# Attention's products in 64x64 tiles of the TensorE array, with dense K and Q

## The chip, the cores and the metric

The kernel runs on one core of a Trainium2 chip. The metric is the device time in microseconds of one execution; the kernel before has a median of 934.84 us over three runs (930.62 to 936.06).

## What is computed

Three stages follow one another: a delta-rule linear attention over 4 batches x 8 heads x 768 tokens x 48 features, a first MoE layer (384 to 1024 and back, SoLU with a layer norm), and a second (384 to 2048 and back, squared ReLU), each over 3072 tokens, all in float32.

```python
def attention(q, k, v, beta):                  # B, H, S, D = 4, 8, 768, 48
    k_n = k / (norm(k) + 1e-6)
    state = zeros(B, H, D, D)
    for t in range(S):
        y[:, :, t] = einsum('bhd,bhde->bhe', q[:, :, t], state)
        v_old = einsum('bhde,bhd->bhe', state, k_n[:, :, t])
        state += beta[:, :, t] * einsum('bhd,bhe->bhde', k_n[:, :, t], v[:, :, t] - v_old)
h = x @ w_in; s = h * softmax(h); x = layernorm(s) * g_ln @ w_out      # first MoE
r = max(x @ w_in2, 0); out = (r * r) @ w_out2                          # second MoE
```

## The kernel before

The sequence of a head is cut into 12 chunks of 64 tokens; 4 batches x 12 chunks are 48 steps, and two steps are one tile of 128 tokens, 24 tiles in all. The 8 heads stand as 4 pairs p, one head h = 0 or 1 of a pair in each half of the 128 partitions (64 tokens of a chunk, or 48 features and 16 unused rows). The unread products of a step, those that don't need the state, are these:

- **E** (`e_tile`, products at L684): K times [Q, K] of the chunk for all heads. K and Q of one step are a load of 96 rows (two heads of 48 features, no gap) x 512 columns from `kine`. Before the products, K is copied into a block-diagonal tile `kbd` or `ez`, one head's 64 columns at a time, each multiplied by a column of ones and zeros (`hm`): on ACT at L673, for half of the first tiles on DVE at L663. Four products of 96x128 weights and 128 moving columns follow, one for each pair, into one PSUM bank (`p_ep`; other free banks for the first seven tiles). ACT takes K x K out as `g` (L693) and DVE the masked K x Q as `m` (L718); `g` goes to DRAM (`gscr`).
- **Inversion** (`inversion`): the 64x64 triangular systems of 7 groups of tiles (2 to 4 tiles each), solved in halves of 32 after a transposing way through DRAM, one system on each of many partitions. Group 0 is on DVE, groups 1 to 6 on POOL (GpSimd); L881 scales the data that come in, L900 and L917 are the steps, L942 scales the result, which goes out to `tscr`.
- **Preparation** (`prep`): loads V (`vt`), the inverses as a block-diagonal `tbd`, and K, Q again in a layout of 64 rows per head with zero rows (`kin`, `kql`, 512 KB a tile). 32x32 products at L1037 and L1050 fill the lower corner of each inverse; they use `p_ep`, and ACT copies it out (L1057, L1068). POOL scales V by the norms (L1079).
- **z** (`zstep`): T times [m, K] of a step, four products of 128x128 weights and 112 columns into `p_z` (L1098), copied out by ACT as `zs` (L1109).

The **chain** (`chain`) is what is read in order, step after step: products of K, Q with the state (L1139, L1140, 48x64 tiles of the array into `p_a` and `p_o`), DVE `r` (L1171), products with `zs` (L1154, L1155), DVE `s` (L1182), ACT `xt` (L1188). A finished tile goes into the first MoE: transposes (L1207), `p_h` (L1218), `p_tr` (L1320), `p_x` (L1340). The second MoE (L1483, L1527) comes last, when all of that is done.

The order on each engine is not that of the code: a planner (`Plan`) takes every operation with an engine, a cost, the keys that it reads and writes, and a priority, and lists them by a list scheduling; `BANKS` names the keys of the PSUM banks. The five engines issue in exactly that order; SyncE (SP) issues all loads and stores. A semaphore wait holds back what stands behind it on its engine. `warm` puts 20 products of a 128x128 identity with itself (L821) on PE between the first E products and the first preparation; they stand behind a late step of inversion 0 in the plan (`late_step`), but read none of its data.

Of the kernel before, what the change touches and what calls it, by code (L numbers as in the profile page):

```python
# [18 lines left out]
P = 128  # L19
C = 64  # L20
# [94 lines left out]
class Plan:  # L115
# [9 lines left out]
    BANKS = {("A", "ep"), ("A", "z"), ("A", "a"), ("A", "o"), ("h", 0), ("h", 1), ("tr",), ("x1",)}  # L125
# [150 lines left out]
def tile_delta_moe_moe(  # L276
# [3 lines left out]
    kin: bass.AP,  # L280
# [45 lines left out]
    hm = cpool.tile([D2, 2], F32, name="hm")  # L326
    idle = cpool.tile([P, 16], F32, name="idle")
# [3 lines left out]
    fac = cpool.tile([P, NT], F32, name="fac")  # L331

# [11 lines left out]
    pool.memset(hm, 1.0)  # L344
    for h in range(2):
        pool.affine_select(
            out=hm[:, h : h + 1],
            in_=hm[:, h : h + 1],
            pattern=[[0, 1]],
            base=1 - D if h else D,  # L350
            channel_multiplier=1 if h else -1,
            compare_op=ALU.is_gt,
            fill=0.0,
        )
# [11 lines left out]
    make_identity(nc, ident)  # L366
# [18 lines left out]
    kbd_ = bufs(ap_, [P, NP, P], "kbd", 2)  # L385
    g_ = bufs(ap_, [P, 2, NP, C], "g", 2)
    sq_ = bufs(ap_, [P, NP, 3, 16], "sq", 2)
    nrm_ = bufs(ap_, [P, GS, NP], "nrm", 3)
    kql_ = bufs(ap_, [P, 2, NP, P], "kql", 2)
    vt_ = bufs(ap_, [P, 2, NP, D], "vt", 2)  # L390
    tbd_ = bufs(ap_, [P, 2 * NP, P], "tbd", 2)
# [17 lines left out]
    p_ep = psA.tile([P, 512], F32, name="p_ep")  # L409
    p_z = psA.tile([P, 512], F32, name="p_z")  # L410
    p_a = psA.tile([P, 512], F32, name="p_a")
    p_o = psA.tile([P, 512], F32, name="p_o")
    p_h = ps1.tile([P, F1], F32, name="p_h")
    p_tr = ps1.tile([P, 512], F32, name="p_tr")
    p_x1 = ps1.tile([P, 512], F32, name="p_x1")
# [7 lines left out]
    for t in (*tbd_, *s_, *g12_):  # L423
        pool.memset(t, 0.0)
# [149 lines left out]

    def rsqrt(y, x, t, n, r, w, prio):
# [38 lines left out]
    def e_tile(t, prio):  # L614
# [15 lines left out]
        for i in range(2):  # L630
            st = 2 * t + i
            kb, kkb = kbd_[i], [("A", "kbd", i)]
            kq, kkq = kqe_[st % 3], [("A", "kqe", st % 3)]
            bank, kep = p_ep, [("A", "ep")]
            if t < LA:

                if st % 6 < 4:
                    kb, kkb = half(ez_[st % 6 // 2], st % 2), [("ezh", st % 6)]
                bank, kep = (
                    (p_h[:, 0:512], [("h", 0)]),  # L640
                    (p_h[:, 512:], [("h", 1)]),
                    (p_tr, [("tr",)]),
                    (p_x1, [("x1",)]),
                    (p_ep, [("A", "ep")]),
                    (p_a, [("A", "a")]),
                    (p_o, [("A", "o")]),
                )[st % (7 if t < T2 else 4)]
# [8 lines left out]
            dma(lambda kq=kq: kq[0:D2], lambda st=st: kine[:, st], (), kkq, prio - 1, D2 * 2048)  # L656
            for h in range(2):
                s = slice(h * C, h * C + C)
                en = "dve" if h and t < T2 else "act"
                fn = (  # L660
                    act.mul
                    if en == "act"
                    else lambda o, x, y: v.tensor_tensor(  # L663
                        out=o,
                        in0=x,
                        in1=y.unsqueeze(2).to_broadcast([D2, NP, C]),
                        op=ALU.mult,
                    )
                )
                add(  # L670
                    en,
                    {"act": c_act(256, True) + 0.09, "dve": c_dve(256)}[en],
                    lambda kq=kq, kb=kb, h=h, s=s, fn=fn: fn(  # L673
                        kb[0:D2, :, s], kq[0:D2, :, C:P], hm[:, h : h + 1]
                    ),
                    kkq,
                    [(*k, h) for k in kkb],
                    prio,
                )
            gp = bank.rearrange("q (p c) -> q p c", p=NP)  # L680
# [5 lines left out]
            r = [*kkq, *((*k, h) for k in kkb for h in range(2))]  # L686
            if kkb[0][0] == "ezh":
                r.append(("ez", st % 6 // 2))
            add("pe", 0.88, mm, r, kep, prio)
# [76 lines left out]
    def gammas(g, prio):  # L766
# [34 lines left out]
        gt = p_z[:, NP * 112 : NP * 112 + HB]  # L801
# [6 lines left out]
        add("pe", 0.22, mm, [kbe], [("A", "z")], prio)  # L808
        add("act", c_act(HB), lambda: act.copy(gm, gt), [("A", "z")], [kgm], prio)

    last_inv = []

    late_step = []

    def warm(n, prio):

        for _ in range(n):

            def mm():
                for i in range(4):  # L820
                    pe.matmul(p_o[:, i * P : i * P + P], ident, ident, start=True, stop=True)  # L821

            add("pe", 0.9, mm, (), [("A", "o")], prio, after=late_step)

    def inversion(g, en, prio):
# [65 lines left out]
        for j in range(1, HB - 1):  # L891
            nr = HB - 1 - j
            for q, (c0, c1) in enumerate(((0, min(j, s1)), (s1, j))):
# [34 lines left out]
                if en == "pool" and run > 0.75:  # L928

                    fn = lambda: pool.memset(idle, 0.0)  # L930
                    brk = [add("pool", 0.1, fn, (), [("idle",)], prio, after=[last])]
                    run = 0.0
# [40 lines left out]
    def prep(t, prio):  # L973
# [7 lines left out]
        kq, vt, tb, t2, g12 = kql_[b], vt_[b], tbd_[b], t2_[b], g12_[b]  # L981
# [18 lines left out]
        for hb in (0, 2, 1, 3):  # L1000
            o = hb * HB
            last = dma(
                lambda o=o: tb[o : o + HB, :, o : o + HB],
# [19 lines left out]
        dma(lambda: kq, lambda: kin[:, 2 * t : 2 * t + 2], (), [("A", "kql", b, i) for i in range(2)], prio - 1, P * 4096)  # L1023

        for i, (bank, kp) in enumerate(((p_ep, "ep"), (p_a, "a")) if t == 0 else ((p_ep, "ep"),)):
# [7 lines left out]
            def mm1(us=us, yp=yp):  # L1033
                for u in us:
                    for h in range(2):
# [4 lines left out]
                            tb[o : o + HB, u, o : o + HB],  # L1040
# [20 lines left out]
            for h in range(2):  # L1061
                o = h * C
                for e in range(2):
# [5 lines left out]
                            tb[o + HB : o + C, us[0] + e : us[-1] + 1 : 2, o : o + HB],  # L1069
# [12 lines left out]
                in1=nrm_[g % 3][:, s0 : s0 + 2].unsqueeze(3).to_broadcast([P, 2, NP, D]),  # L1082
                op=ALU.mult,
            ),
            [("A", "nrm", g % 3, s) for s in (s0, s0 + 1)],
# [25 lines left out]
    def chain(st, prio):  # L1111
# [17 lines left out]
        def lower(h):  # L1129
            return slice(h * C, h * C + C)  # L1130
# [565 lines left out]
```

## Time and profile before

| | before |
|---|---|
| median of 3 runs | 934.84 us |
| the profiled execution | 934.67 us |
| its span in the trace | 932.7 us |
| busy: PE / DVE / ACT / POOL | 864.9 / 519.5 / 487.3 / 365.2 us |
| DMA | 101.75 MB, 109 GB/s mean |

PE is TensorE's matmul, PEld its weight load, SPq the queue of SyncE that issues DMAs. A matmul of float32 leaves two records in the trace, so an E step of four products has 8. Records of matmuls overlap, since they are pipelined: the pace is read from one start to the next. PEclk is the granted clock of TensorE as a share of full speed; 1.00 and 0.50 are its two levels (2.4 and 1.2 GHz). Some instructions wait for a semaphore, and "[10.85 <-DMA tbd<-tscr]" behind a row says how long the engine was idle before it and what ended this.

### The profile page before, as it was taken

How to read it: one execution, taken by the hardware profiler on the slowest of the kernel's cores; microseconds unless marked ns; L12 is line 12 of the kernel's file. 1: busy time of each engine (PE TensorE's matmuls, PEld its weight loads, DVE VectorE, ACT ScalarE, POOL GpSimd, SP SyncE). 2: the span in 40 equal slices, each digit the busy share in tenths (PEclk: the TensorE clock that was granted, in tenths of full speed). 3: DMA queues.
4: the chain of work that ended last, by engine and by line, in shares of the span. 5: the costliest groups of instructions: out<-in, count | busy, mean ns of one | idle time of the engine just before them, and what ended most of it. 6: DMA issues, size and time to landing. Idle time of an engine off the chain costs nothing.

```text
span 932.7 us, 23189 instructions
## 1 busy us (share of the span) xinstructions
PE 864.9 (93%) x9144; PEld 806.9 (87%) x9144; DVE 519.5 (56%) x1063; ACT 487.3 (52%) x1069; POOL 365.2 (39%) x898
## 2 busy tenths in 40 slices
PE   7349789989998999999998999999999999999998
PEld 6347678867887888888887999999999999999998
DVE  6996887786856896634435655343343434343332
ACT  5335787666756766666565644333333434343333
POOL 6399889899747947987500000000000000000000
PEclk8566898989998999999999999999999999999999
DMA  8827876858687577442314432001010101000000
GB/s 243 212 85 192 202 225 177 231 169 235 201 221 198 144 226 184 120 143 68 101 44 136 132 106 63 15 6 47 1 51 1 51 1 52 1 26 1 26 1 26
DMA packets 129244, 101.75 MB, mean 109 GB/s; under 512 B 84080, under 2 KB 106608, under 8 KB 129136
## 3 DMA queue, kind: packets, MB, share of 16 engines
q1 hardware_dynamic: 129136, 100.28, 38.4%
q8 instruction: 72, 1.18, 0.6%
q14 instruction: 36, 0.29, 0.1%
HBM read 70.88 MB, written 29.36 MB: 107 GB/s over the span
## 4 chain that ended last, share of the span: by engine, by line
PE 70%; DVE 8%; POOL 8%; DMA 7%; SPq 2%; ACT 2%; issue 2%; POOLq 0%; ACTq 0%; DVEq 0%
PE acc L1527 22%; PE h L1483 21%; PE p_x L1340 8%; PE p_h L1218 7%; PE p_z L1098 3%; POOL it L917 2%; POOL itmp L900 2%; SPq L300 2%; PE p_tr L1320 2%; PE p_a L1139 2%; DVE itmp L900 1%; DVE it L917 1%; DMA vt<-in_vtok_dram 1%; PE p_ep L684 1%; DMA m<-in_ktok_dram 1%
## 5 line engine op out<-in xcount | busy, mean ns | idle before, releaser
L1504 DVE TENSOR_TENSOR xt<-xt 128x384 f32<-128x384 f32 x128 | 71.5, 559 | 163.7 <-ACT xt L1496 163.5
L1496 ACT ACTIVATE xt<-h 128x384 f32<-128x384 f32 x128 | 62.9, 492 | 167.8 <-PE h L1483 167.7
L1483 PE MATMUL h<-x1h,w2h 128*128 128x384 f32 x384 | 128.9, 336 | 0.0
L1483 PE MATMUL h<-x1l,w2h 128*128 128x384 f32 x384 | 128.6, 335 | 0.0
L1483 PE MATMUL h<-x1h,w2l 128*128 128x384 f32 x384 | 128.3, 334 | 0.0
L917 POOL TENSOR_TENSOR it<-it,itmp 128x72 f32<-128x72 f32 (+37 forms) x255 | 110.1, 446 | 5.1
L900 POOL TENSOR_TENSOR itmp<-it 128x72 f32<-128x72 f32 (+37 forms) x255 | 109.3, 443 | 1.9
L1527 PE MATMUL acc<-woh,xl 128*128 128x384 f32 x258 | 87.4, 339 | 0.0
L1527 PE MATMUL acc<-wol,xh 128*128 128x384 f32 x258 | 87.3, 338 | 0.0
L1340 PE MATMUL p_x<-zh,wgh 128*128 128x256 f32 x288 | 85.7, 298 | 1.5 <-ACT xo L1354 1.5
L1527 PE MATMUL acc<-woh,xh 128*128 128x384 f32 x258 | 86.9, 337 | 0.0
L1340 PE MATMUL p_x<-zl,wgh 128*128 128x256 f32 x288 | 81.5, 283 | 1.0 <-DVE zl L433 1.0
L1340 PE MATMUL p_x<-zh,wgl 128*128 128x256 f32 x288 | 81.6, 283 | 0.0
L433 DVE TENSOR_TENSOR xl<-xt,xh 128x384 fp32r<-128x384 f32 x86 | 48.0, 558 | 45.7 <-ACT xh L428 45.5
L1483 PEld LDWEIGHTS h<-x1h,w2l 128*128 128x128 f32 x384 | 72.1, 188 | 0.0
L1483 PEld LDWEIGHTS h<-x1h,w2h 128*128 128x128 f32 x384 | 72.1, 188 | 0.0
L1483 PEld LDWEIGHTS h<-x1l,w2h 128*128 128x128 f32 x384 | 72.1, 188 | 0.0
L428 ACT CAST xh<-xt 128x384 fp32r<-128x384 f32 x86 | 44.1, 513 | 47.8 <-DVE xt L1504 46.7
L1218 PE MATMUL p_h<-w1h,xh 128*128 128x512 f32 x144 | 65.0, 451 | 0.1
L1098 PE MATMUL p_z<-m,tbd 128*128 128x112 f32 x384 | 59.9, 305 | 0.7 <-ACT tbd L1068 0.5
L1218 PE MATMUL p_h<-w1h,xl 128*128 128x512 f32 x144 | 59.1, 410 | 0.1
L1218 PE MATMUL p_h<-w1l,xh 128*128 128x512 f32 x144 | 58.8, 408 | 0.0
(197 smaller groups left out, 2152.0 us busy)
## 6 DMA issues: line engine op xcount, KB each, us to landing
kql<-in_kin_dram SPq DMA_DIRECT2D x24, 512.0 KB
kqe<-in_kine_dram SPq DMA_DIRECT2D x40, 192.0 KB
raw<-in_w2i_dram SPq DMA_DIRECT2D x12, 512.0 KB
raw<-in_w2o_dram SPq DMA_DIRECT2D x16, 384.0 KB
gscr<-g SPq DMA_DIRECT2D x21, 256.0 KB
m<-in_ktok_dram SPq DMA_DIRECT2D x24, 192.0 KB
vt<-in_vtok_dram SPq DMA_DIRECT2D x24, 192.0 KB
x1scr<-xo SPq DMA_DIRECT2D x12, 384.0 KB
```

Source lines behind the costliest of these rows:

```text
L300: return add("sp", 0.06, lambda: nc.sync.dma_start(dst(), src()), r, w, prio, size, gate)
L428: add("act", c_act(n), lambda: act.copy(hi(), src()), r, [w[0]], prio)
L433: lambda: le.tensor_tensor(out=lo(), in0=src(), in1=hi().bitcast(F32), op=ALU.subtract),
L900: lambda tm=tm, j=j, nr=nr, w_=w_, c0=c0, c1=c1: eng.tensor_tensor(out=tm, in0=it[:, j + 1 :, j : j + 1].to_broadcast([P, nr, w_]), in1=it ...
L917: lambda tm=tm, j=j, c0=c0, c1=c1: eng.tensor_tensor(out=it[:, j + 1 :, c0:c1], in0=it[:, j + 1 :, c0:c1], in1=tm, op=ALU.add,),
L1098: pe.matmul(zp[:, p].rearrange("q (j c) -> q j c", j=7), tb[:, i * NP + p], m[:, i, :, p], start=True, stop=True,)
L1218: pe.matmul(p_h[:, sl], xx[:, c], ww[:, c, sl], start=(c == 0 and k == 0), stop=(c == 2 and k == 2),)
L1340: pe.matmul(p_x1[:, 0 : 2 * P], ww[:, f, c * P : c * P + P], zz[:, f], start=(f == 0 and k == 0), stop=(f == 7 and k == 2),)
L1483: pe.matmul(late["h2", ih], late[ww][:, c, s], xx[:, c], start=(c == 0 and k == 0), stop=(c == 2 and k == 2),)
L1496: lambda: act.activation(out=rt, in_=late["h2", ih], func=AF.Relu),
L1504: lambda: v.tensor_tensor(out=gg, in0=rt, in1=rt, op=ALU.mult),
L1527: pe.matmul(late["acc", a], gg[:, a * P : a * P + P], late[ww][:, f], start=(f == 0 and k == 0), stop=(f == 15 and k == 2),)
```

## The change

- **E**: 8 products a step with 48x64 weights, one for each head, in place of four. The array is used as four 64x64 tiles: the rows are those of the head (0 to 47 or 64 to 111), and the columns are the same half for pairs 0 and 1, the other half for pairs 2 and 3 (`CROSS_PAIRS`). K and Q are read as loaded; the copies `kbd`, `ez` and `hm` are gone. Each step is loaded in two halves of 48 rows.
- **z**: 8 products of 64x64 weights and 112 columns a step. The inverses lie compact (`t_`, 64 columns a head, in place of `tbd` with 128).
- **Banks**: E and z of a step write the same pair of banks, x and y (pairs 0, 1 and 2, 3), E to the first 128 columns of a pair, z behind it. The preparation and the small products of `gammas` use x too. The first seven tiles of E use pairs of banks of the other stages.
- **Crossed data**: what belongs to pairs 2 and 3 has its heads in the other half of the partitions. K by tokens and beta are laid out so on the host; the norms that scale V are crossed back by three small ACT copies a group (`nrx`).
- **Loads of the chain**: `kin` is gone; `kql` comes from `kine` in two halves of 48 rows.
- **Warm-up**: 24 products in place of 20, and the moving operand is `idle`, 128x128, which DVE writes behind step 29 of inversion 0. `idle`'s former role, a small memset on POOL between steps, goes to `brk`.

```diff
-    BANKS = {("A", "ep"), ("A", "z"), ("A", "a"), ("A", "o"), ("h", 0), ("h", 1), ("tr",), ("x1",)}
+    BANKS = {("A", "x"), ("A", "y"), ("A", "a"), ("A", "o"), ("h", 0), ("h", 1), ("tr",), ("x1",)}
...
+    p_xy = psA.tile([P, 1024], F32, name="p_xy")
+    p_ao = psA.tile([P, 1024], F32, name="p_ao")
+    p_tx = ps1.tile([P, 1024], F32, name="p_tx")
+    xy = p_xy.rearrange("q (p c) -> q p c", p=NP)
+    KXY = [("A", "x"), ("A", "y")]
...
+    CROSS_PAIRS = [(j + 2 * k, k, h) for j in range(2) for k in range(2) for h in range(2)]
...
+                banks, kep = (
+                    (p_h, [("h", 0), ("h", 1)]),
+                    (p_tx, [("tr",), ("x1",)]),
+                    (p_xy, KXY),
+                    (p_ao, [("A", "a"), ("A", "o")]),
+                )[st % (4 if t < T2 else 2)]
+            else:
+                banks, kep = p_xy, KXY
...
-            dma(lambda kq=kq: kq[0:D2], lambda st=st: kine[:, st], (), kkq, prio - 1, D2 * 2048)
             for h in range(2):
+                dma(
+                    lambda kq=kq, h=h: kq[feats(h)],
+                    lambda st=st, h=h: kine[h * D : h * D + D, st],
...
-                    lambda kq=kq, kb=kb, h=h, s=s, fn=fn: fn(
-                        kb[0:D2, :, s], kq[0:D2, :, C:P], hm[:, h : h + 1]
-                    ),
...
-            def mm(kq=kq, kb=kb, gp=gp):
-                for p in range(NP):
-                    pe.matmul(gp[:, p], kb[0:D2, p], kq[0:D2, p], start=True, stop=True)
...
+            def mm(kq=kq, gp=gp):
+                for p, cross, h in CROSS_PAIRS:
+                    pe.matmul(
+                        gp[toks(h ^ cross), p],
+                        kq[feats(h), p, C:P],
+                        kq[feats(h), p],
+                        start=True,
+                        stop=True,
                     )
...
-            add("pe", 0.88, mm, r, kep, prio)
+            add("pe", 0.5, mm, r, kep, prio)
...
-                    pe.matmul(p_o[:, i * P : i * P + P], ident, ident, start=True, stop=True)
-
-            add("pe", 0.9, mm, (), [("A", "o")], prio, after=late_step)
+                    pe.matmul(p_o[:, i * P : i * P + P], ident, idle, start=True, stop=True)
+
+            add("pe", 0.9, mm, [("idle",)], [("A", "o")], prio)
...
-                        late_step.append(mul)
+                        fn = lambda: v.memset(idle, 1.0)
+                        brk = [add("dve", 0.2, fn, (), [("idle",)], prio, after=[mul])]
...
-        zp = p_z[:, 0 : NP * 112].rearrange("q (p c) -> q p c", p=NP)
-        tb, m, zs = tbd_[t % 2], m_[t % LA], zs_[i]
+        zp = xy[:, :, P : P + 112]
+        tb, m, zs = t_[t % 2], m_[t % LA], zs_[i]
 
         def mm():
-            for p in range(NP):
+            for p, cross, h in CROSS_PAIRS:
+                q = toks(h ^ cross)
                 pe.matmul(
-                    zp[:, p].rearrange("q (j c) -> q j c", j=7),
-                    tb[:, i * NP + p],
-                    m[:, i, :, p],
+                    zp[toks(h), p].rearrange("q (j c) -> q j c", j=7),
+                    tb[q, i * NP + p],
+                    m[q, i, :, p],
...
-        add("act", c_act(448), lambda: act.copy(zs, zp), [("A", "z")], [("A", "zs", i)], prio)
+        add("act", c_act(448), lambda: act.copy(zs, zp), KXY, [("A", "zs", i)], prio)
...
-    warm(5, -55)
+    warm(6, -55)
```

The planner lays the order of every engine anew. On PE, between the last E of the start (`p_x` before, `p_tx` after) and the first preparation (`g_0` is the data of group 0 from `gscr`, `tbd` or `t` the inverses), there stood before:

```order
L684 MATMUL p_x_231<-kqe_183,ez_164 128x128 [waits DMAHW1_49,Activation_49]
L684 MATMUL p_x_231<-kqe_183,ez_164 128x128 x3
L821 MATMUL p_o<-ident 128x128 x20
L1037 MATMUL p_ep<-tbd_198,g_0_202 32x32 [waits DMAHW7_49,DMAHW2_49]
L1037 MATMUL p_ep<-tbd_198,g_0_202 32x32 [waits DMAHW3_49,DMAHW0_49]
```

And now:

```order
L666 MATMUL p_tx<-kqe_180 64x128 [waits DMAHW5_49,Activation_49]
L666 MATMUL p_tx<-kqe_180 64x128 [waits DMAHW6_49]
L666 MATMUL p_tx<-kqe_180 64x128 x6
L828 MATMUL p_ao<-idle,ident 128x128 [waits DVE_49]
L828 MATMUL p_ao<-idle,ident 128x128 x23
L1053 MATMUL p_xy<-t_196,g_0_200 32x32 [waits DMAHW4_49]
```

The warm-up keeps its place and now begins with a wait for DVE; the E step waits for two loads, and no longer for a copy of its own.

On PE in the middle, where tile 7 is prepared, an E step and a z step stood side by side between products of the first MoE (`p_h`), each on a bank of its own:

```order
L1218 MATMUL p_h<-w1h,xl_160 128x512
L684 MATMUL p_ep<-kqe_184,kbd_185 128x128 [waits DMAHW6_49,Activation_49]
L684 MATMUL p_ep<-kqe_184,kbd_185 128x128 x3
L1098 MATMUL p_z<-m_179,tbd_199 128x112 [waits DMAHW7_49,DMAHW6_49]
L1098 MATMUL p_z<-m_179,tbd_199 128x112 x3
L1218 MATMUL p_h<-w1h,xh_158 128x512
```

Now a z step of the same stretch reads:

```order
L1351 MATMUL p_tx<-zl,wgh 128x256
L1115 MATMUL p_xy<-m_176,t_197 64x112 [waits DVE_49]
L1115 MATMUL p_xy<-m_176,t_197 64x112 x7
L1053 MATMUL p_xy<-t_196,g_0_200 32x32 [waits DMAHW3_49,Activation_49]
L1053 MATMUL p_xy<-t_196,g_0_200 32x32 [waits DMAHW4_49]
L1053 MATMUL p_xy<-t_196,g_0_200 32x32 x14
L1165 MATMUL p_ao<-r_206,zs_204 48x48 [waits DVE_49]
```

z and the preparation follow each other directly on the same banks, with the wait for ACT's copy of z between them and the chain (L1165) behind.

On SP at the start, between the stores of `gscr` (its parts 75 and 76 are groups 0 and 1) and the loads of inversion 1's data (`it`), there stood:

```order
L300 DMA gscr_76<-g_188 128x512
L300 DMA gscr_76<-g_187 128x512
L300 DMA kqe_184<-in_kine_dram 96x512
L300 DMA kqe_182<-in_kine_dram 96x512
L300 DMA vt_196<-in_vtok_dram 128x384
L300 DMA kqe_183<-in_kine_dram 96x512
L300 DMA g_0_202<-gscr_75 32x8x32 x2
L300 DMA kql_194<-in_kin_dram 128x1024
L300 DMA raw_221<-in_w1i_dram 128x1024
L300 DMA raw_222<-in_w1i_dram 128x1024
L300 DMA it_213<-gscr_76 24x32x32 x4
```

And now:

```order
L299 DMA gscr_76<-g_182 128x512
L299 DMA kqe_181<-in_kine_dram 48x512 x2
L299 DMA kql_192<-in_kine_dram 48x1024
L299 DMA gscr_76<-g_183 128x512
L299 DMA kql_192<-in_kine_dram 48x1024
L299 DMA kqe_180<-in_kine_dram 48x512
L299 DMA m_176<-in_ktok_dram 128x2x192
L299 DMA m_177<-in_ktok_dram 128x2x192
L299 DMA m_178<-in_ktok_dram 128x2x192
L299 DMA kqe_179<-in_kine_dram 48x512 x2
L299 DMA it_211<-gscr_76 24x32x32 x4
```

Behind the first store shown, four loads of K and Q stood ahead of `it` (the one of 128x1024 in the layout with zero rows); now there are seven, each of 48 rows, and three loads of K by tokens (`m`).

## Rows read from the trace of the kernel before

**Rows 1.** The page: its first line

```profile
span 932.7 us, 23189 instructions
```

**Rows 2.** By stage: stretch, length, busy PE/PEld/DVE/ACT/POOL, PEclk, DMA share, GB/s

```profile
63.00:80.00 17.00, 9.14 (x192) 7.68 (x196) 12.10 (x19) 8.25 (x23) 16.97 (x33) 0.50 0.64 170
80.00:165.00 85.00, 74.98 (x1197) 64.31 (x1190) 67.15 (x134) 66.64 (x156) 78.87 (x171) 0.84 0.75 200
165.00:250.00 85.00, 77.59 (x1165) 67.86 (x1163) 65.12 (x108) 59.12 (x135) 79.83 (x201) 0.96 0.72 202
250.00:350.00 100.00, 92.92 (x1428) 79.99 (x1418) 75.94 (x161) 64.52 (x154) 60.25 (x153) 0.97 0.73 206
350.00:525.00 175.00, 170.50 (x2635) 149.46 (x2634) 86.01 (x180) 108.09 (x232) 91.36 (x271) 0.99 0.43 117
525.00:932.00 407.00, 404.09 (x2340) 403.51 (x2338) 159.45 (x279) 154.38 (x305) 0.00 (x0) 1.00 0.09 30
```

**Rows 3.** Timeline of POOL: start, duration, line, tile, idle time before

```profile
43.89 6.38 POOL L881 TENSOR_TENSOR it<-it,gm 128x1024 f32<-128x1024 f32 x1 [9.29 <-DMA it<-gscr]
```

**Rows 4.** POOL's last big step per inversion: min/median/max ns, first and last start

```profile
L942 POOL TENSOR_TENSOR it<-it,gm x6: 1914/1916/2422, 123.9 to 452.1; 128x1024 f32<-128x1024 f32 x6
```

**Rows 5.** The chain that ended last, up to 130 us: start, duration, what

```profile
3.12 0.43 SPq L300
...
31.43 1.22 DVE it L881
...
59.45 0.46 DVE itmp L900
```

**Rows 6.** Timeline of PE, 336 to 340 us: start, duration, line, product

```profile
336.55 1.06 PE L684 MATMUL p_ep<-kqe,kbd 96*128 96x128 f32 x8
337.44 1.04 PE L1098 MATMUL p_z<-m,tbd 128*128 128x112 f32 x8
338.41 0.25 PE L1139 MATMUL p_a<-s,kql 48*64 48x48 f32 x1
...
338.56 0.22 PE L1139 MATMUL p_a<-s,kql 48*64 48x48 f32 x1
...
338.62 0.22 PE L1139 MATMUL p_a<-s,kql 48*64 48x48 f32 x1
...
339.02 0.38 PE L1340 MATMUL p_x<-zh,wgh 128*128 128x256 f32 x1
```

**Rows 7.** E by stage: stretch, length, busy PE (records), PEld, PEclk, DMA, GB/s

```profile
80.00:165.00 85.00, 14.24 (x80) 12.73 (x80) 0.84 0.75 200
165.00:525.00 360.00, 19.56 (x144) 17.86 (x144) 0.98 0.58 162
```

**Rows 8.** z by stage, columns as in rows 7

```profile
80.00:165.00 85.00, 15.88 (x80) 14.38 (x80) 0.84 0.75 200
165.00:525.00 360.00, 39.91 (x288) 35.09 (x288) 0.98 0.58 162
```

**Rows 9.** Tile p_ep, 100-350 us: its evacuation; who waited, us, times

```profile
L693 ACT ACTIVATE g<-p_ep x26: 359/384/396, 99.8 to 344.5; 128x256 f32<-128x256 f32 x26
...
  PE p_ep L1037: 4.2, 2
  PE p_ep L684: 4.0, 5
...
  PE p_ep L1050: 1.0, 1
```

**Rows 10.** Groups by line: tile, count, busy us, mean ns, idle before

```profile
L673 ACT ACTIVATE kbd<-kqe,hm 96x256 f32<-96x256 f32 x61 | 29.4, 504 | 6.9 <-DMA kqe<-in_kine_dram 6.7
...
L1109 ACT COPY zs<-p_z 128x448 f32<-128x448 f32 x48 | 25.4, 528 | 10.2 <-PE p_z L1098 10.0
```

**Rows 11.** Timeline of PE at the first preparation, columns as in rows 6

```profile
68.21 0.75 PE L1037 MATMUL p_ep<-tbd,g 32*32 32x32 f32 x13 [10.85 <-DMA tbd<-tscr]
...
71.89 2.06 PE L1098 MATMUL p_z<-m,tbd 128*128 128x112 f32 x8 [0.29 <-ACT tbd L1068]
```

More of the change, by code (lines that the diff above doesn't have):

```diff
@@ L325, in tile_delta_moe_moe @@
     mask = cpool.tile([P, C], F32, name="mask")
-    hm = cpool.tile([D2, 2], F32, name="hm")
-    idle = cpool.tile([P, 16], F32, name="idle")
+    idle = cpool.tile([P, P], F32, name="idle")
+    brk_ = cpool.tile([P, 16], F32, name="brk")
     sm_all = cpool.tile([P, NT], F32, name="sm_all")
@@ L331, in tile_delta_moe_moe @@
     fac = cpool.tile([P, NT], F32, name="fac")
-    cst = cpool.tile([P, 6], F32, name="cst")
-    cst_u = cst.bitcast(U32)
-    for i, x in enumerate((TINY, 1.0, 1e-6, F64_HI)):
-        v.memset(cst[:, i : i + 1], x)
-    v.memset(cst_u[:, 4:5], 0x7FFFFFFF)
-    v.memset(cst_u[:, 5:6], 0x3FFFFFF8)
-    def const(i, n, u=False):
-        return (cst_u if u else cst)[:, i : i + 1].to_broadcast([P, n])
[L344 to L354, printed above, removed]
     pool.memset(mask, 1.0)
@@ L366, in tile_delta_moe_moe, with const @@
     make_identity(nc, ident)
+    cst = cpool.tile([P, 6], F32, name="cst")
+    cst_u = cst.bitcast(U32)
+    for i, x in enumerate((TINY, 1.0, 1e-6, F64_HI)):
+        v.memset(cst[:, i : i + 1], x)
+    v.memset(cst_u[:, 4:5], 0x7FFFFFFF)
+    v.memset(cst_u[:, 5:6], 0x3FFFFFF8)
+    def const(i, n, u=False):
+        return (cst_u if u else cst)[:, i : i + 1].to_broadcast([P, n])
     wgh = m1.tile([P, 8, DM], F32R, name="wgh")
@@ new lines, in e_tile @@
+            gp = banks.rearrange("q (p c) -> q p c", p=NP)[:, :, 0:P]
+            def mm(kq=kq, gp=gp):
[6 more added lines that the diff above has]
+                        stop=True,
+                    )
+            r = [(*k, h) for k in kkq for h in range(2)]
+            if kkq == [("junk",)]:
+                r.append(("junk",))
@@ L799, in gammas @@
         dv(lambda: v.tensor_tensor(out=b, in0=b, in1=y, op=ALU.mult), [ky], [kbe])
-        gt = p_z[:, NP * 112 : NP * 112 + HB]
+        nx = nrx_[g % 3]
+        knx = [("A", "nrx", g % 3, i) for i in range(3)]
+        ns = nrm_[g % 3]
+        add("act", c_act(16, True), lambda: act.copy(nx[:, 0:n, 0:2], ns[:, 0:n, 0:2]), kn, [knx[2]], prio)
+        for h in range(2):
+            add(
+                "act",
+                c_act(16, True),
+                lambda h=h: act.copy(nx[toks(h), 0:n, 2:4], ns[toks(1 - h), 0:n, 2:4]),
+                kn,
+                [knx[h]],
+                prio,
+            )
+        gt = xy[:, 0:2, 240:256]
         def mm():
@@ L928, in inversion @@
                 if en == "pool" and run > 0.75:
-                    fn = lambda: pool.memset(idle, 0.0)
-                    brk = [add("pool", 0.1, fn, (), [("idle",)], prio, after=[last])]
+                    fn = lambda: pool.memset(brk_, 0.0)
+                    brk = [add("pool", 0.1, fn, (), [("brk",)], prio, after=[last])]
                     run = 0.0
@@ L1022, in prep @@
                 )
-        dma(lambda: kq, lambda: kin[:, 2 * t : 2 * t + 2], (), [("A", "kql", b, i) for i in range(2)], prio - 1, P * 4096)
-        for i, (bank, kp) in enumerate(((p_ep, "ep"), (p_a, "a")) if t == 0 else ((p_ep, "ep"),)):
+        for h in range(2):
+            dma(
+                lambda h=h: kq[feats(h)],
+                lambda h=h: kine[h * D : h * D + D, 2 * t : 2 * t + 2],
+                (),
+                [("A", "kql", b, i, h) for i in range(2)],
+                prio - 1,
+                D * 4096,
+            )
+        for i, (bank, kp) in enumerate(((p_xy, "x"), (p_a, "a")) if t == 0 else ((p_xy, "x"),)):
             us = range(i * NP, i * NP + NP) if t == 0 else range(2 * NP)
@@ L1166, in chain @@
         else:
-            add("pe", 0.5, mm_a, [("A", "kql", t % 2, i), ks], [("A", "a"), ("A", "o")], prio)
+            add("pe", 0.5, mm_a, [*(("A", "kql", t % 2, i, h) for h in range(2)), ks], [("A", "a"), ("A", "o")], prio)
             add(
```

114 lines of the change are left out of this document (42 added, 72 removed).

## The prediction

> **What bounds the kernel now.** The profiled execution took 934.67 us with a span of 932.7 [rows 1], so 1.97 us lie outside the span; the median of the runs shown is 934.84, and I sum against 934.7 throughout. First I read the table by stage [rows 2]. Behind 525 us the second MoE fills PE without a break (404.1 of 407 us), and nothing of the change is there. Between 165 and 525 us PE is busy 77.6 + 92.9 + 170.5 = 341 of 360 us, 95%: attention and the first MoE share one engine, and work taken off it moves the end forward. Between 80 and 165 us PE is busy 75 of 85 us at a granted clock of 0.84, and POOL 78.9 of 85: POOL's inversion of group 1 starts at 43.89 us [rows 3], and its last big step starts at 123.9 [rows 4]. The tiles of group 1 can't begin before. The start, up to 80 us, is a chain of loads, E products and the DVE inversion of group 0, which begins at 31.43 us [rows 5].
>
> **The change part by part.** *E products.* The rows of PE around 336 us show one E step of four 128-wide products (8 records) starting at 336.55 and the next work at 337.44, so 0.89 us, 0.111 per record of 128 columns [rows 6]. For the new form the chain products are the model, since they are already 48x64 and 64x64 tiles: their records start in fours, one for each tile, at 338.56, at 338.62 and so on, so 0.06 us for four records of 48 columns [rows 6]. A record of 128 columns took 0.111, that is 0.87 ns a column, so 48 columns need 0.042 us, and the pace of 0.06 is rather that of the weights (64 columns; beside the matmuls). Four tiles do run at once: one after the other, two records alone would need 0.083. An E step becomes 8 products, 16 records, four rounds of four. The lower bound is 4 x 0.111 = 0.44 us, the upper 0.89 (two tiles at a time); I take 0.44, since it comes from rows of the same form. *z products.* A z step started at 337.44, the chain behind it at 338.41, so 0.97, of which 8 x 0.111 = 0.89 are its own and 0.08 the change to smaller tiles [rows 6]. The new one needs 4 x 112 x 0.87 ns = 0.39 (bounds 0.24, the pace of the weights, and 0.89); I take 0.40. Counted behind 80 us, there are 80 + 144 = 224 records of E, 28 steps [rows 7], and 80 + 288 = 368 of z, 46 steps [rows 8]. Saved: 28 x 0.45 = 12.6 and 46 x 0.49 = 22.5, together **35.1 us** of PE.
>
> *Changes of tile size.* Entering small tiles costs the 0.08 above. Leaving: the 32 records of the chain from 338.41 need 8 x 0.058 = 0.46, and the next product starts at 339.02, so 0.15 is lost [rows 6]. In PE's order such changes rise from 256 to 301, because the steps stand between products of the first MoE as often as beside the chain. 45 x 0.115 = **+5.2 us** (bounds 3.6 and 6.8).
>
> *Shared banks.* Before, E and the preparation of T used p_ep, z had p_z for itself. Now all of them use the pair x, y, and the next user waits until ACT and DVE have emptied it; behind the waiting product everything on PE's queue waits, the chain too. Between 100 and 350 us the instructions that use p_ep kept PE waiting 4.2 + 4.0 + 1.0 = 9.2 us over 26 E steps and the preparations of 13 tiles, two uses each: 52 uses, 0.18 per use [rows 9]. I charge 0.18 to each of the 46 z, which used to have a bank to themselves: **+8.3 us**. The lower bound is 0, if other products always stand between; the upper 30, if each of the 122 uses (28 E, 46 z, 48 of preparation) waits twice as long as a use of p_ep does now: 122 x 0.36 less the 76 x 0.18 of today.
>
> PE's work so falls by 35.1 - 5.2 - 8.3 = 21.6 us. Of the 35.1, 18 x 0.45 + 36 x 0.49 = 25.7 (73%) lie behind 165 us [rows 7, 8], where PE is busy 95%; the rest where the chain waits for POOL, and there I count half. 21.6 x (0.73 x 0.95 + 0.27 x 0.5) = **17.9 us** off the end.
>
> *The block-diagonal copies of K* go: on ACT alone 61 of one form take 29.4 us at 0.504 each [rows 10], and DVE made half of them at the start. In the middle ACT is busy only 62 to 78% [rows 2], so there I count nothing; the relief would show in quicker evacuations, which is inside the bounds above, and without that cover it would be worth no more than it measures. Added on ACT: three small copies of the norms per group, under 21 x 0.504 = 10.6 us, under the same cover. At the start each E step loses the copy between its load and its products. Against this each load becomes two: SP issues one in 0.43 us [rows 5], so 8 more for group 0 are 3.4 us of SP, and ia, the data of inversion 0, stands behind them. In DVE's order the first product of inversion 0 now stands ahead of most of group 1's norms. Bounds -6 and +4 us; I take **-2**, since inversion 1 on POOL, which its own 9.29 us wait for data starts [rows 3], need not follow.
>
> *Loads.* K and Q come without zero rows: 24 loads of 512 KB become 48 of 192, and 48 of 192 become 96 of 96, so 72 issues more, 31 us of SP over 500 us, and 3 MB less. In SP's order loads of the next steps stand ahead of the data of inversion 1. I count 0, with up to +5 if POOL's waits grow.
>
> *Warm-up products.* Before, the 40 records end at 57.4, and PE then idles 10.85 us until 68.21; the z step of 71.89 takes 2.06 us, more than twice 0.89, as the clock stands at 0.50 from 63 to 80 us [rows 2, 11]. Now 48 records wait for a DVE write behind one of the last products of inversion 0, near 59 us [rows 5], and end between 5.3 (48 x 0.111) and 10.7 us later, so about when the first T arrives. That saves about 1 us on each of the first two z steps, and I count 0, since tile 4 waits for inversion 1 in any case; without that cover it is -2, or +2 if the warm-ups end after T's arrival.
>
> Sum: 934.7 - 17.9 - 2 = 914.8, forecast **915**.
>
> **The rivals.** *POOL holds the front back* (0.15): POOL is busy 78.9 and then 79.8 of 85 us up to 250 [rows 2], and if its inversions set the pace till there, what lies ahead of 250 counts for nothing: of 0.73 x 21.6 = 15.8 us behind 165, spread over its 360 us, 275/360 remain, 12.1, times 0.95: 11.5 us, so 923. Against it: from 250 to 350 us POOL works only 60.3 of 100 us and PE 92.9, so PE, not POOL, was behind by then. *Everything is real* (0.12): no bank waits, PE bound throughout, 6 us at the start: 35.1 - 5.2 + 6 gives 899. *The clock falls* (0.09): PE is left emptier, and if 165 to 350 us ran at the 0.84 of the stage before instead of 0.96 and 0.97 [rows 2], 185 x 0.125 = 23 us would be lost, which eats the gain: 938. The lower of its two levels (1.2 and 2.4 GHz) was granted throughout 63 to 80 us, behind an idle stretch of 10.85 us [rows 2, 11]. *The shared pair of banks becomes the limit* (0.09, the case on the other side): the saving of 35.1 - 5.2 = 29.9 over 74 steps is 0.40 us each, and from there on the change loses. A z step's evacuation alone takes 0.528 [rows 10]; at 0.55 per step it is 40.7 - 29.9 = 10.8, times 0.83, 9 us more: 944. Against it: today's 0.18. *Tiles in one bank follow one another* (0.05): the products of the two row halves of a pair write the same bank, and if these couldn't run together, E and z would keep 0.89, and 13.5 x 0.83 = 11 us come on top: 946. The rows speak against it: the four chain products write p_a from both row halves and keep 0.06 a round [rows 6]. The Trainium skill, "TensorEngine Tiling (Array Packing)", section "Restrictions and Gotchas", states it as a rule that different row tiles can't use the same PSUM bank at once; by that rule the steps would run two tiles at a time and the sum would be the 946 of this rival, while the trace disagrees for 48 columns; no row shows 128. That the warm-ups don't wait would change 2 us at most, and is within the forecast.
>
> **How the numbers follow.** Forecast 0.50; 923 with 0.15, 899 with 0.12, 938 with 0.09, 944 with 0.09, 946 with 0.05. About 0.5% is what a measurement of this kernel can tell from no change: faster than 930.2 are the first three, 0.77; within, the clock's case and a little of its neighbours, 0.10; slower, 0.13. The range is 899 to 939: it leaves out the two slow cases (0.14) and half of the case at 899.
>
> **What would show it.** Right: an E step of 0.44 and a z step of 0.40 us from start to next start, four records in a round; the second MoE beginning some 20 us earlier with PE no emptier between 165 and 500 us; ACT's work down by some 30 us; a z step near 72 us at full clock. Wrong: rounds of two records (the bank rule), waits of PE for ACT zs and DVE m of over 30 us in sum (the banks), more stretches at the low clock, or a last inversion on POOL whose last big step starts as late as its 452.1 us of now [rows 4].

## The result

The changed kernel takes 948.1 us (median of four runs, 942.1 to 952.2) against 934.5: a ratio of 1.0139 with a 95% interval of 1.0098 to 1.018, slower, and above the range of 899 to 939. The profiled execution took 942.1 us with a span of 940.4; it is the fastest of the four, so the trace shows 7.7 us of the longer span and not the 13.6 of the medians. The head of the page, with the clock's line (40 equal slices, granted clock in tenths):

```profile
span 940.4 us, 24790 instructions
...
PE 846.3 (90%) x9920; PEld 759.1 (81%) x9920; DVE 511.9 (54%) x1050; ACT 460.7 (49%) x1008; POOL 355.2 (38%) x895
...
PEclk7565679999799999999999999999999999999999
```

PE has less to do, 846.3 us against 864.9, in a longer span. The same stages as in [rows 2] (stretch, length, busy PE, PEld, DVE, ACT, POOL, granted clock, DMA share, GB/s):

```profile
63.00:80.00 17.00, 8.87 (x272) 7.24 (x272) 6.02 (x11) 7.25 (x24) 14.27 (x37) 0.59 0.62 155
80.00:165.00 85.00, 69.21 (x1218) 51.94 (x1214) 74.22 (x125) 57.85 (x130) 75.43 (x154) 0.76 0.69 181
165.00:250.00 85.00, 73.20 (x1291) 58.97 (x1284) 61.60 (x113) 47.36 (x111) 75.85 (x200) 0.94 0.72 203
250.00:350.00 100.00, 94.44 (x1650) 75.29 (x1651) 75.63 (x170) 66.97 (x158) 69.22 (x173) 0.95 0.69 189
350.00:525.00 175.00, 158.15 (x2755) 131.51 (x2754) 81.39 (x166) 103.66 (x224) 89.10 (x267) 0.98 0.42 112
```

From 350 to 525 us PE is busy 158.2 of 175, where it was 170.5: it stands. POOL's last big steps [rows 4] begin no earlier than before, 126.2 against 123.9 at the first of its inversions, 455.7 against 452.1 at the last:

```profile
L950 POOL TENSOR_TENSOR it<-it,gm x6: 1912/1914/2317, 126.2 to 455.7; 128x1024 f32<-128x1024 f32 x6
```

The products themselves are as fast as forecast. In PE's timeline an E step (L666) and a z step (L1115), each in one row of 16 records, and what comes next:

```profile
330.26 0.67 PE L666 MATMUL p_xy<-kqe 48*64 48x128 f32 x16
330.86 0.50 PE L1229 MATMUL p_h<-w1h,xh 128*128 128x512 f32 x1
```

```profile
299.76 0.61 PE L1115 MATMUL p_xy<-m,t 64*64 64x112 f32 x16
300.31 0.50 PE L1229 MATMUL p_h<-w1h,xh 128*128 128x512 f32 x1
```

E takes 0.60 and z 0.55 us to the next product, with the change of tile size, where [rows 6] have 0.89 and 0.97. What stands against that is seen in another group: the products of the first MoE's output, which had 1.5 us of idle time ahead of them before, now have 14.5. The first line is of the kernel before, the second of the changed one (busy us, mean ns | idle before, what ended it):

```profile
L1340 PE MATMUL p_x<-zh,wgh 128*128 128x256 f32 x288 | 85.7, 298 | 1.5 <-ACT xo L1354 1.5
L1351 PE MATMUL p_tx<-zh,wgh 128*128 128x256 f32 x288 | 88.8, 308 | 14.5 <-DVE xl L424 3.9 <-DVE zl L424 3.7 <-ACT zh L419 3.4
```

These products read `zh` and `zl` and write the second half of `p_tx`. `xl` is none of their data: DVE makes it out of the transposes in the first half. Of all waits of p_x and p_tr products in the built program (p_x is the name of the output in the second half, tile `p_x1`), 33 are for an instruction that touches only the other half; before, with two tiles `p_tr` and `p_x1`, there was none.

To add up where PE's time went, I count from the start of each PE record to the start of the next, idle time apart, behind 80 us (us; the last three columns are kernels of the next section):

| | before | changed | b_tx | a_split | b_less |
|---|---|---|---|---|---|
| E | 30.3 | 18.7 | 30.0 | 18.6 | 19.5 |
| z | 49.4 | 26.1 | 49.4 | 26.7 | 28.2 |
| chain, preparation | 78.5 | 77.8 | 80.0 | 78.9 | 83.2 |
| first MoE | 259.2 | 279.2 | 266.2 | 270.4 | 269.7 |
| second MoE | 402.2 | 403.2 | 402.3 | 402.5 | 402.3 |
| idle | 29.0 | 51.3 | 34.4 | 39.1 | 41.3 |

E and z give 34.9 us. The first MoE, whose work is untouched, takes 20.0 more, and PE idles 22.3 more. Of the 20.0, 8.5 are in products that lie in a stretch granted the low clock by the trace (18.2 us over their pace, against 9.7 before). At the full clock 4.0 more are in products that a smaller tile follows, 4.0 in products that follow one, and 3.9 in the products next to a wait. At both clocks together, the products of the first MoE that a smaller tile follows were 8.0 us over their own pace before, 77 of them, and are 13.4 now, 126: 5.4 more, at about 0.1 us each before and now. Another 28 were followed by E or z before, which had the whole array then, and lost next to nothing.

### The profile page after: what moved, and what is told of

The parts are those of the page before. It is cut to its first block, busy times and chain, and to the rows that moved or that the text cites. A ratio compares the mean times of both kernels' runs of the same rounds, so it can differ in the third digit from the quotient of the medians.

```text
span 940.4 us, 24790 instructions
## 1 busy us (share of the span) xinstructions
PE 846.3 (90%) x9920; PEld 759.1 (81%) x9920; DVE 511.9 (54%) x1050; ACT 460.7 (49%) x1008; POOL 355.2 (38%) x895
## 4 chain that ended last, share of the span: by engine, by line
PE 72%; DVE 10%; ACT 7%; DMA 5%; SPq 3%; issue 3%; POOL 1%; DVEq 0%; ACTq 0%; POOLq 0%
PE acc L1538 22%; PE h L1494 21%; PE p_tx L1351 9%; PE p_h L1229 9%; SPq L299 3%; PE p_tx L1331 2%; PE p_xy L666 2%; PE p_xy L1115 2%; DVE it L925 1%; DVE itmp L907 1%; PE p_ao L1150 1%; ACT xt L1199 1%; PE p_ao L1166 1%; DMA raw<-in_w1i_dram 1%; DVE zl L424 1%
## 5 line engine op out<-in xcount | busy, mean ns | idle before, releaser
L1515 DVE TENSOR_TENSOR xt<-xt 128x384 f32<-128x384 f32 x128 | 71.5, 558 | 169.6 <-ACT xt L1507 169.4
L1351 PE MATMUL p_tx<-zh,wgh 128*128 128x256 f32 x288 | 88.8, 308 | 14.5 <-DVE xl L424 3.9
L1351 PE MATMUL p_tx<-zh,wgl 128*128 128x256 f32 x288 | 81.2, 282 | 0.0
L1351 PE MATMUL p_tx<-zl,wgh 128*128 128x256 f32 x288 | 81.1, 282 | 0.0
L1351 PEld LDWEIGHTS p_tx<-zh,wgh 128*128 128x128 f32 x288 | 54.1, 188 | 25.5 <-DVE zl L424 7.3
L1229 PE MATMUL p_h<-w1h,xh 128*128 128x512 f32 x144 | 69.3, 481 | 1.9 <-ACT xh L419 1.4
L1229 PE MATMUL p_h<-w1h,xl 128*128 128x512 f32 x144 | 61.5, 427 | 1.2 <-DVE xl L424 1.1
L1229 PE MATMUL p_h<-w1l,xh 128*128 128x512 f32 x144 | 61.6, 428 | 0.0
```

The costliest lines, as they stand in the source:

```text
L1229: pe.matmul(p_h[:, sl], xx[:, c], ww[:, c, sl], start=(c == 0 and k == 0), stop=(c == 2 and k == 2),)
L1351: pe.matmul(p_x1[:, 0 : 2 * P], ww[:, f, c * P : c * P + P], zz[:, f], start=(f == 0 and k == 0), stop=(f == 7 and k == 2),)
L1515: lambda: v.tensor_tensor(out=gg, in0=rt, in1=rt, op=ALU.mult),
```

## The experiments

Times are compared with runs of the kernel before on the same chip (932 to 933 us). Names with b_ start from the kernel before, a_ from the changed one, s_ from a_split.

**b_tx**: the merged tile alone, in the kernel before.

```diff
-    p_tr = ps1.tile([P, 512], F32, name="p_tr")
-    p_x1 = ps1.tile([P, 512], F32, name="p_x1")
+    p_tx = ps1.tile([P, 1024], F32, name="p_tx")
+    p_tr, p_x1 = p_tx[:, 0:512], p_tx[:, 512:]
```

> The kernel before, with one change: p_tr and p_x1 (transposes of the first MoE, its output) are the two halves of one tile of two banks, p_tx, as in the changed kernel. Nothing else. In the built order 37 more products of PE then wait for the emptying of the half that they don't use. Theory A (the changed kernel loses because the two halves of p_tx wait for each other): slower by 10 to 20 us, 945 to 955, with PE idle ahead of p_x and p_tr up from 11 us to over 20. Theory B (the loss is from the pair x, y, or from the clock at the start, or from the inversions on POOL): 933 to 937, no change.

Measured: 947.9 us, ratio 1.0149 (1.0122 to 1.0177), as much as the whole change. The order of all engines is that of before, 37 waits for the other half are added, and the group of p_x shows them, with `xl` and `xh` among the releasers:

```profile
L1340 PE MATMUL p_tx<-zh,wgh 128*128 128x256 f32 x288 | 88.1, 306 | 16.4 <-DVE zl L433 7.0 <-DVE xl L433 5.1 <-ACT xh L428 2.8
```

So theory A holds in the old kernel: this edit alone costs 14 to 15 us. The idle time ahead of all p_x and p_tr products behind 80 us rises from 10.6 to 21.9 us, as theory A has it. Other idle time falls meanwhile, so that the column of idle rises by only 5.4 us; 7.0 more are in the first MoE, 4.3 of them at the low clock and 2.9 in the products next to a wait.

**a_split**: the changed kernel with the two tiles apart.

```diff
-    p_tx = ps1.tile([P, 1024], F32, name="p_tx")
+    p_tr = ps1.tile([P, 512], F32, name="p_tr")
+    p_x1 = ps1.tile([P, 512], F32, name="p_x1")
...
                     (p_h, [("h", 0), ("h", 1)]),
-                    (p_tx, [("tr",), ("x1",)]),
                     (p_xy, KXY),
                     (p_ao, [("A", "a"), ("A", "o")]),
-                )[st % (4 if t < T2 else 2)]
+                )[st % (3 if t < T2 else 2)]
```

> The changed kernel, with p_tr and p_x1 as two tiles again; the E products of the start take three pairs of banks in turn in place of four (two of p_h, x y behind tile T2). Theory A: the forecast's saving comes out, 915 to 930. Theory B (x, y or the start's clock): 942 to 952, as the changed kernel. Theory C (POOL's inversions hold the front, whatever PE does): 930 to 936, the last inversion on POOL still starts at 390 to 396 us.

Measured: 928.1 us, ratio 0.9943 (0.9914 to 0.9972): faster than both. Each against its own runs of before, it lies 5.1 us below, where the changed kernel lies 13.6 above. No wait of p_x and p_tr for the other half is left:

```profile
L1350 PE MATMUL p_x<-zh,wgh 128*128 128x256 f32 x288 | 87.2, 303 | 3.1 <-ACT xo L1364 2.9 <-issue 0.2
```

But of the 34.4 us that E and z save here, 5 arrive; in the table the first MoE takes 11.2 more than before and PE idles 10.1 more. A wait shows that the kernel before hardly had, z for ACT's copies of the lower corner of T (first line before, second a_split):

```profile
L1098 PE MATMUL p_z<-m,tbd 128*128 128x112 f32 x384 | 59.9, 305 | 0.7 <-ACT tbd L1068 0.5
L1114 PE MATMUL p_xy<-m,t 64*64 64x112 f32 x768 | 32.0, 283 | 14.9 <-ACT t L1083 13.1 <-DVE m L705 1.0 <-ACT zs L1125 0.7
```

Those copies fill what z reads and empty bank x, which z writes; which of the two it waits for can't be told here. Behind 80 us E, z and the preparation together stand 22.5 us in a_split, where it was 11.8 before.

The change also makes one tile, `p_ao`, out of the two of the chain, and a_split leaves it so. In the built program 15 waits of its products (16 in the changed kernel, none before) are for ACT's copy `xt` out of the `p_o` half, while the product writes the `p_a` half. In the trace the group now stands for `xt` (first line before, second a_split):

```profile
L1139 PE MATMUL p_a<-s,kql 48*64 48x48 f32 x704 | 31.5, 228 | 1.9 <-DVE s L1182 1.9
L1149 PE MATMUL p_ao<-s,kql 48*64 48x48 f32 x704 | 32.3, 235 | 6.1 <-ACT xt L1198 5.6 <-DVE s L1192 0.4
```

What this pair costs was not tried alone.

**The warm-up.** b_warm is the kernel before with the new warm-up alone; a_warm is the changed kernel with the old one (the lines on `warm`, `late_step` and `idle` of the diff above, applied or taken back); a_nowait leaves everything of the changed kernel in its order but the wait:

```diff
-                    pe.matmul(p_o[:, i * P : i * P + P], ident, idle, start=True, stop=True)
+                    pe.matmul(p_o[:, i * P : i * P + P], ident, ident, start=True, stop=True)
```

> The kernel before with the new warm-up alone: 24 products that wait for a DVE write behind step 29 of inversion 0. Forecast's step: 0 to -2 us (932 to 935), the z step near 72 us at 0.9 us in place of 2.06. Rival: the products end later than the inverses arrive, +2 us, or the clock of the next stretches falls, +5 us and more.

> The changed kernel with the warm-up products of before (20, identity with itself, no wait for DVE's data). If the data-dependent warm-up is worth what the forecast says, within 2 us of the changed kernel (946 to 950). If it shifts the clock of the start (0.58 of 80 to 120 us in the changed kernel, 0.76 to 0.82 before), 938 to 944.

> The changed kernel, in the same order, with warm-up products that multiply the identity with itself, so that they stand at the same place and wait for nothing. If the 10 us that the changed kernel lost with the old warm-up come from the wait (the clock after it), 954 to 960; if they come from the other order that the planner made, 945 to 950.

Measured: b_warm 935.3 (0.9988 to 1.005), a_warm 958.6 (1.0208 to 1.0306), a_nowait 950.2 (1.0129 to 1.022). The wait is worth nothing that can be measured, in either kernel. The 10 us of a_warm above the changed kernel are not the wait, since a_nowait has none either; that leaves the order that the planner made for it and its 20 products in place of 24, which weren't tried apart.

**What an order is worth.** Four kernels leave the work of a_split or of before as it is and tell the planner other costs, so that only the order differs:

```diff
-            add("pe", 0.5, mm, r, kep, prio)
+            add("pe", 0.88, mm, r, kep, prio)
...
-    CROSS = 0.2
+    CROSS = 0.35
```

The first pair is s_cost (z's 0.45 likewise to 0.86); s_true has 0.6 and 0.54 there, b_order 0.99 and 0.98 in the code of before. The second pair is s_cross.

> a_split with the planner told the old costs of E and z (0.88 and 0.86 us in place of 0.5 and 0.45), so that it lays more other work behind each. Nothing is different on the chip but the order. If the gain of a_split (5 us) is held down by PE standing before the next product of the same step for ACT's copies (z for the corner of T: 12.3 us, against 0.2 before), more work between lets it out: 918 to 925. If it is held by POOL's inversions or by the chain, 926 to 932.

> a_split with the planner told the measured paces of E and z (0.60 and 0.54 us to the next product, in place of 0.5 and 0.45). Only the order differs. If the planner's estimate is what keeps the gain back, 918 to 925; if orders of about the same quality scatter as s_cost did, anywhere in 924 to 938.

> a_split with the planner's charge for a result that crosses to another engine raised from 0.2 to 0.35 us, so that it puts other work between the products of the preparation, ACT's copies and z. Only the order differs. If PE's 10 us of standing before z are what is lost, they fall below 5 and the time to 918 to 924; if not, 924 to 932.

> The kernel before, with the planner told the paces of the trace for its own E and z (0.99 and 0.98 us to the next product, in place of 0.88 and 0.86). Only the order differs. It shows what a new order alone moves: within 3 us of before if orders are worth little, up to 8 either way if the scatter of s_cost is common.

Measured: s_cost 935.7 (1.0001 to 1.0053), s_true 932.5 (0.9963 to 1.0028), s_cross 930.9 (0.996 to 1.0014), b_order 933.4 (0.998 to 1.0036). In s_cross PE's standing before z behind 80 us fell to 5.7 us, from 10.2 in a_split, and before the chain and the first MoE it rose from 16.6 to 25.1: the time went elsewhere. No order let the gain out, and the new form lies between 928 and 936 in five orders (with s_pad below), by -1.3 us from before on the mean. So the 5 us of a_split may be its order. A difference of under 8 us between two kernels with different orders says nothing of the edit.

**s_pad**: K and Q loaded with zero rows again, in as many loads as before (for E here, for the chain likewise).

```diff
-            for h in range(2):
-                dma(
-                    lambda kq=kq, h=h: kq[feats(h)],
-                    lambda st=st, h=h: kine[h * D : h * D + D, st],
+            dma(
+                lambda kq=kq: kq,
+                lambda st=st: kine[:, st],
```

> a_split with K and Q loaded with their 16 zero rows per head, one load a step for E and one a tile for the chain, as many loads as before the change (72 fewer than a_split, 20% to 33% more bytes in each). If the halved loads cost nothing (the forecast's step), 925 to 931, as a_split. If the further loads on SP hold back the start and POOL's data, up to 5 us less, 921 to 925; the E products of the start would then begin earlier (step 8 at 18.5 us in a_split, 14.8 before).

Measured: 929.4 us (0.9946 to 1.0012), like a_split: the 72 further loads cost nothing that shows beyond what an order makes.

**Who holds the front.** Here work is left out or doubled in an unchanged order. b_half and s_half shrink the steps of the inversions on POOL to one column; b_less leaves out two of four products; b_both does both; s_double makes each new product twice.

```diff
-                        in1=it[:, j : j + 1, c0:c1].to_broadcast([P, nr, w_]),
+                        in1=it[:, j : j + 1, c0 : c1 if en == "dve" else c0 + 1].to_broadcast(
...
-                for p in range(NP):
+                for p in range(NP if t <= LA else 2):
...
-                for p, cross, h in CROSS_PAIRS:
+                for p, cross, h in CROSS_PAIRS * (1 if t < LA else 2):
```

> The kernel before, in its own order, with the inversions on POOL shrunk: each of their steps works on one column in place of up to 22 (most of the inversion is left out, everything else is done). Theory C (POOL's inversions hold the front up to some 455 us): well over 15 us faster, below 918. Theory P (PE's own work holds it, 95% busy): 928 to 935.

> a_split (two tiles for p_tr and p_x1) in its own order, with the inversions on POOL shrunk in the same way (most of the inversion is left out). Theory C: the saving of PE, 31 us by the paces of the trace, now comes out: 20 us or more below the shrunk kernel before. Theory P: some 5 us below it, as without the shrinking, and PE then waits for the latencies between its own products and ACT's copies, which a shorter inversion doesn't touch.

> The kernel before, in its own order, with half of the products of E (tiles 11 to 23) and of z (all but the first two steps) left out: two pairs of four. PE is given back 26 x 0.445 + 46 x 0.445 = 32 us, as much as the 64x64 tiles save, with no new change of tile size, no new order, no shared bank. Theory P, on which the forecast rests (PE, 95% busy behind 165 us, holds the front): 905 to 912. Theory L (the front is held by latencies between PE, ACT, DVE, POOL and DMA, and PE's busy share is work that fills in): 922 to 930.

> Both cuts at once in the order of before: half of E's and z's products left out, and the inversions on POOL on one column each. Theory P: PE's 32 us come out on top of the 7 of the shrunk inversion, 893 to 905. If PE and POOL hold the front in turns: the sum of the two single gains or more. Theory L (latencies): 915 to 922, little more than the shrunk inversion's 926.

> a_split in its own order with each product of E (tiles 10 to 23) and of z made twice: 28 x 0.44 + 48 x 0.39 = 31 us of PE put back, with the same changes of tile size and the same waits. Theory P: up by 25 to 30, 953 to 958. Theory L: up by 3 to 10, 931 to 938, the gain that the smaller tiles had brought.

Measured, with the ratio to before:

| | us | ratio, 95% interval | change, us |
|---|---|---|---|
| b_half (POOL less) | 925.8 | 0.9884 to 0.9949 | -7.4 |
| b_less (PE less) | 930.3 | 0.9934 to 0.9997 | -2.6 |
| b_both | 915.0 | 0.9761 to 0.9829 | -17.9 |
| s_half | 921.6 | 0.984 to 0.9918 | -11.6 |
| s_double | 942.2 | 1.0069 to 1.0161 | +9.3 |

b_less is the forecast's own claim put to the test: 32 us of PE taken off, with no other edit, bring 2.6. With POOL relieved too, the same 32 us bring 10.5 (b_half to b_both), and the two cuts together bring 17.9, more than the 10.0 that they bring apart. That fits PE and POOL holding the front in turns, and theories P and C are wrong as put. It isn't shown alone: theory L (latencies between the engines) forecast 922 to 930 and 915 to 922 for b_less and b_both, and both measurements lie at the edge of that. Nor does it hold for the new form: s_half lies 4.2 us below b_half, as a_split lies 5.1 below before, so relieving POOL lets out no more of its 34 us. The stages of b_less show the second place where the time goes (columns as above, with [rows 2] beside them):

```profile
80.00:165.00 85.00, 75.22 (x1202) 61.49 (x1198) 71.80 (x140) 69.14 (x163) 78.74 (x176) 0.77 0.76 205
165.00:250.00 85.00, 71.56 (x1056) 60.82 (x1051) 64.45 (x105) 55.67 (x128) 76.88 (x196) 0.90 0.70 197
250.00:350.00 100.00, 88.25 (x1320) 73.92 (x1313) 74.62 (x161) 64.32 (x154) 61.56 (x156) 0.92 0.74 211
350.00:525.00 175.00, 168.91 (x2592) 146.77 (x2591) 88.44 (x184) 111.29 (x239) 89.98 (x268) 0.99 0.41 116
```

The granted clock fell from 0.84, 0.96 and 0.97 to 0.77, 0.90 and 0.92, and PE idles 12.3 us more (the table above). The first MoE, in the same order with the same work, takes 10.5 us longer, all of it in products at the low clock (20.5 us over their pace there, against 9.7). In b_both the clock is partly back, at 0.86, 0.92 and 0.95:

```profile
80.00:165.00 85.00, 72.67 (x1239) 60.04 (x1234) 70.06 (x151) 70.68 (x170) 57.72 (x169) 0.86 0.78 208
165.00:250.00 85.00, 74.29 (x1078) 62.74 (x1078) 61.36 (x113) 56.65 (x128) 49.80 (x187) 0.92 0.73 217
250.00:350.00 100.00, 91.87 (x1501) 77.78 (x1501) 72.86 (x163) 68.22 (x166) 51.74 (x185) 0.95 0.75 209
```

s_double goes the other way: 31 us of PE put back into a_split cost 14, not 31, and the low clock recedes: 43 us of it behind 80 us, where a_split has 65, before 44 and b_less 77. It has about as much E and z on PE as the kernel before (75.6 us against 79.7), and lies 9.3 us above it. What stands out there against before are the changes of tile size (13.1 against 8.0 us) and PE standing ahead of z (8.6 us against 0.4); but its order is another too, and an order alone made up to 8.

## Why the prediction was wrong

- **E and z** were sized right in sum: 35.1 us were forecast, 34.9 are there. In part that is luck: on the mean behind 80 us E went from 1.08 to 0.67 us a step and z from 1.07 to 0.57, so both forms took some 0.2 longer than the sum has it (0.89 to 0.44 and 0.40), and the difference stayed. Four tiles run at once with 128 columns too. The rule that I weighed there, in the Trainium skill, "TensorEngine Tiling (Array Packing)", section "Restrictions and Gotchas", that different row tiles can't use one bank at the same time, would have given 0.89 us a step; the trace disagrees, with 0.60. (Of the four chain records that the prediction cites against it, two write p_a and two p_o.)
- **Changes of tile size**: forecast 5.2 us. The first MoE shows 5.4 more in products that a smaller tile follows and, at the full clock, 4.0 more in products that follow one; what the ends of E and z themselves cost is inside the 34.9. The term was too small, and that its first part is near 5.2 is chance.
- **Shared banks** is the step that failed first. It priced the pair x, y at 8.3 us, and in the changed kernel E, z and the preparation stand 9.3 us behind 80 us, no more than their 11.8 of before; in a_split they stand 10.7 more, near the price. The diff makes two more pairs out of single banks, and one of them, `p_tx`, joins two tiles that had worked side by side, the transposes and the output of the first MoE. I read it only as a place for the first E products. The planner keeps a key for each half and lays the order as if they were free of each other; the program's waits go by the tile. It cost 14.8 us in the order of before (b_tx), and it was in the diff to be seen: count whose waits change when a tile grows, not only who writes it newly.
- **The weight** of the saving failed next. The sum took 0.95 of what lies behind 165 us for gain, because PE was busy 95% there. b_less measured 2.6 of 32 us. A busy share says that little time is idle; it doesn't say that what is freed isn't filled by the next wait or by a lower clock. The rows spoke of it: POOL was busy 78.9 and 79.8 of 85 us up to 250, and its last big step stood at 452.1 us [rows 2, 4]. The rival "POOL holds the front back" had a part of it, but I let it act up to 250 us alone; POOL's last big step is at 452.1, 455.7 and 450.1 us in before, the changed kernel and b_less.
- **The clock falls** was a rival for 23 us, and it is a part of the answer in b_less and in the changed kernel (0.76, 0.94 and 0.95 against 0.84, 0.96 and 0.97). In b_less and s_double, each in the order of its own start, the low clock came with less work on PE and went with more. The five orders of the new form have 62 to 77 us of it behind 80 us (a_split, s_cost, s_true, s_cross, s_pad), before, b_order and b_warm 38 to 49. Whether the waits bring the low clock or the low clock shifts the waits, no run here separates.
- **The start** did gain: the inversion of group 0 begins at 27.2 us in place of 31.4, and the first products of the chain on `zs` at 71.5 in place of 74.6. But the inversion on POOL had to wait 12.55 us for its data, up to 46.58, where [rows 3] have 9.29; the step itself then took 2.37 us in place of 6.38, and ended no later:

```profile
46.58 2.37 POOL L888 TENSOR_TENSOR it<-it,gm 128x1024 f32<-128x1024 f32 x1 [12.55 <-DMA it<-gscr]
```

- **Loads and warm-up** were put at nothing, and no run shows otherwise (s_pad, b_warm, a_nowait). The sign that I named for the warm-up did not come true: the first z step still runs at the low clock, with 1.02 us where it is 0.61 later.

```profile
56.63 6.45 PE L828 MATMUL p_ao<-idle,ident 128*128 128x128 f32 x45
64.92 0.63 PE L1053 MATMUL p_xy<-t,g 32*32 32x32 f32 x13 [1.84 <-DMA t<-tscr]
...
68.97 1.02 PE L1115 MATMUL p_xy<-m,t 64*64 64x112 f32 x16 [0.72 <-ACT t L1084]
```

- The idle stretch of PE ahead of the first preparation did shrink from 10.85 us to 1.84; no run shows a gain from it.
- The rivals at 944 and 946 lie near the measured 948.1, but by luck: for the first the pair x, y would have had to stand longer in the changed kernel, and for the second its tiles to run two at a time, and neither is so.

What stays open: how the rest of the 32 to 35 us, which doesn't arrive in b_less and a_split, divides among order, clock and waits; what the pair `p_ao` costs; and why a_warm is 10 us worse.

## What to carry to other kernels

When two tiles become halves of one, ask for each of them what it now waits for, and try that edit alone: here it cost 14.8 us, more than the faster products brought in any order that was tried. Before work is taken off a busy engine, leave half of it out in an unchanged order; two lines told that 32 us of PE are worth 3 here, and 10 with a second engine relieved. Where a planner lays the order anew, differences below what a change of its costs alone makes (8 us here) can't be given to the edit.

## What the runs showed of the hardware

- Four 64x64 tiles ran together although two row halves wrote one bank: 16 records of 128 columns in 0.60 us, where eight of 128 columns on the whole array took 0.89.
- With less work, PE was granted less: 0.90 and 0.92 in place of 0.96 and 0.97 in the middle stages, in the same order (b_less). With more work in the order of a_split it was granted more: 43 us at the low clock behind 80 us in place of 65 (s_double).
- A product of the first MoE on the whole array that a smaller tile follows took some 0.1 us over its pace, before (8.0 us, 77 times) and with the 64x64 E and z among them (13.4 us, 126 times).
